# Hashed attention with a feed-forward layer on one core: the first token casts moved up, a load drawn forward, and two more output units summed by DMA

## The chip, the core and the metric

The kernel runs on one core of a Trainium2 chip. The core has five engines with a queue of instructions each: TensorE (PE in the profile), VectorE (DVE), ScalarE (ACT), GpSimd (POOL) and SyncE (SP, which here only issues DMAs). An engine takes its queue in order, so an instruction that waits holds up all that stands behind it. The metric is the device time of one execution in microseconds (us), less is better.

## What is computed

Attention over 4 batches of 8 heads, 768 tokens of 64 numbers each, in which a query sees the keys of its own hash bucket alone, and then a feed-forward layer on all 3072 tokens:

```python
q_bits = (np.einsum('bhsd,dk->bhsk', q, proj) > 0)      # 6 bits, k likewise
mask = q_bucket[:, :, :, None] == k_bucket[:, :, None, :]
scores = np.where(mask, scale * np.matmul(q, k.transpose(0, 1, 3, 2)), -1e9)
attn = np.exp(scores - max); attn = attn / (sum + 1e-09)
x = (attn @ v) as (3072, 512)                           # tokens x (head, dim)
h = x @ w_in                                            # 512 x 2048
out = (h * np.clip(h + 3.0, 0.0, 6.0) / 6.0) @ w_out    # 2048 x 512
```

Inputs and outputs are float32.

## The kernel before

**Precision.** Every matmul works on pairs: a number is rounded (ACT, a cast to fp32r, the high part) and the rest is a subtraction (the low part), and products of high with high, high with low and low with high are added up. So the attention weights p become `ph` (L475) and `pl` (L477 on POOL, L479 on DVE), a token chunk `xr` becomes `xh` (L642) and `xl` (L643).

**Attention.** The 32 heads have 6 tiles of 128 queries each: 192 steps, numbered k or g, head 16 having steps 96 to 101. For a step, TensorE computes scores against all keys (L387, L389), three steps ahead (`lead`), DVE takes the maximum (L396, in `lowest`), ACT the exponential (L408), TensorE transposes p (L418), ACT and DVE split it, and TensorE multiplies with the values into an accumulator `acc` (L500, L512). From step 102 on, p goes by DVE's transposition (L429, "flip") and a round trip by DMA through the tensors `fd`, `spare` and `px`. The hash bits of a head come from six matmuls `z` (L334 to L336) and a comparison on DVE (L352, `bits`). A head's queries and keys (`raw`) are cast and split on POOL two heads ahead (L276, L304, L318). The tile they are written to is the one that the scores of two heads before are computed from.

**Outputs.** An accumulator holds two query tiles (a unit u = 0, 1 or 2 of a head, 256 tokens) as two halves of 64 partitions that have to be summed. `output` copies it whole to a tile `y` (ACT, L542), units 0 and 1 to a tile y0, unit 2 to y2; both tiles exist once (`bufs=1`). The first half is stored to the tensor `xs` by a plain DMA, and the second half added to it there by a DMA of GpSimd that accumulates (`add`, L521). `add` is called in steps with k+3 at 1 or 4 of a head's six, and later on at k at 1 or 3. For the last head of a batch, all three units (of batch 0 the third alone) are summed on the chip instead: ACT copies one half (L539), DVE adds the other (L540), and one store does.

**Feed-forward.** `xs` holds attention before division by the sums. The FFN of batch 0 runs by itself from step 52 on; those of batches 1 to 3 run beside attention from step 101 on (`beside_ffn`), in chunks (b, t) of 256 tokens. A chunk is loaded (`load_x`, four groups of 128 columns, two heads each), the reciprocals of the sums are spread (L570 on POOL), transposed (`rt`, L580, on TensorE), multiplied in (L583, DVE) and the result is split (`split_x`). `there` says when a chunk may begin: when its units are out and no addition to its batch is held. The first chunk, (1, 0), is prepared in steps 94 to 101 and split at the start of step 102 (`opening`), and then TensorE computes h (L653), ACT and DVE the activation (L675, L676) and its split (L681, L682, the operand `gb`), and TensorE the product with w_out (`po`, L691 to L696).

**Order.** PE, DVE, ACT and POOL run in the order in which the code is written, step by step. SP's DMAs are put in order by the framework, which also adds the semaphore waits: for data, and for tiles that are reused. `bank` takes a PSUM bank that an earlier tile has to leave.

The lines are those of the kernel before; in the changed one the same instructions stand 6 or 7 lines lower (L546 for L542, L576 for L570, L586 for L580, L649 for L642). L521 is the same in both.

Of the kernel before, what the change touches and what calls it, by code (L numbers as in the profile page):

```python
# [10 lines left out]
F32 = mybir.dt.float32  # L11
# [7 lines left out]
P = 128  # L19
# [9 lines left out]
LA = 3  # L29
# [14 lines left out]
def lsh_attention_moe(  # L44
# [11 lines left out]
    B, H, D, S = qkT.shape  # L56
    D //= 2
    DM, DF = w_in.shape
    KT = S // P
    HW = S // 2  # L60
    QT = HW // P
    NCC = DM // P
    NFC = DF // P
    TC = 256
# [5 lines left out]
    sp = ctx.enter_context(tc.tile_pool(name="sp", bufs=2))  # L70
# [5 lines left out]
    def dma(out: bass.AP, in_: bass.AP):  # L76
        nonlocal last
        last = nc.sync.dma_start(out=out, in_=in_)
# [4 lines left out]
    spare = []  # L83

    def wide_tile(shape, dtype, name: str):
        nonlocal ob_turn
        tag = "oa" if spare else ("oa", "ob")[ob_turn % 2]
        ob_turn += 1
        return sp.tile(shape, dtype, name=name, tag=tag, bufs=1)
# [301 lines left out]
    def lowest(g: int):  # L391

        s = scs.pop(g)
        m = sp.tile([P, 1], F32, name=f"m{g}", tag="m", bufs=4)
        pr_ = sp.tile([P, 2, HW], F32, name=f"p{g}", tag="p", bufs=2)
        nc.vector.tensor_scalar(  # L396
            out=pr_[:], in0=s[:, :, :HW], scalar1=CAP, scalar2=None,
            op0=ALU.min, op1=ALU.min, accum_out=m[:],
        )
        probs[g] = pr_, m  # L400
# [113 lines left out]
                    start=(part == 0 and kt == 0), stop=(part == 1 and kt == KT - 1),  # L514
                )

    adds = []

    def add():
        for _, to, of in adds:  # L520
            nc.gpsimd.dma_start(out=to, in_=of, accum_op=ALU.add)  # L521
        adds.clear()

    def output(un: int):
        nonlocal vdone
        i, u = divmod(un, KT // 2)
        b, h = divmod(i, H)
        o = (h % 2) * D
        acc = accs.pop(un)

        if u != 1:
            outs[i] = sp.tile([P, 4 * P if u == 0 else 2 * P], F32, name=f"y{i}_{u}", tag=f"y{u}", bufs=1)
        y = outs[i][:, 2 * P :] if u == 1 else outs[i][:, : 2 * P]

        r = slice(o, o + D)
        r2 = slice(D - o, 2 * D - o)
        last_head = h == H - 1 and (b > 0 or u == 2)
        if last_head:
            nc.scalar.copy(y[r], acc[r2])  # L539
            nc.vector.tensor_add(y[r], acc[r], y[r])  # L540
        else:
            nc.scalar.copy(y, acc[:])  # L542
        if u or last_head:
            c = slice(2 * u * P, 2 * (u + 1) * P) if last_head and b else slice(0, 4 * P) if u == 1 else slice(4 * P, S)
            to = xs[b][h * D : (h + 1) * D, c]

            with tc.issue_after(copied.ins):
                dma(out=to, in_=y[r] if last_head else outs[i][r])
            if not last_head:
                adds.append((i, to, outs[i][r2]))  # L550
        vdone = 2 * un + 2


# [44 lines left out]
        if pieces:  # L598
            pieces.pop(0)()

    def load_x(b: int, t: int, ccs: range):
        assert all(not b * H <= a[0] < b * H + ccs.stop * P // D for a in adds)
        ts = slice(t * TC, (t + 1) * TC)
        xr = wide_tile([P, NCC, TC], F32, f"xr{b}_{t}")
        of = xs[b][: len(ccs) * P, ts].rearrange("(cc p) t -> p cc t", p=P)
        if paced:
            for cc in ccs:
                pieces.append(lambda cc=cc: dma(out=xr[:, cc], in_=of[:, cc]))
            piece()
        else:  # L610
            dma(out=xr[:, : len(ccs)], in_=of)
        return xr

    def scale_x(b: int, t: int, ccs: range, xr, rc=None):
# [132 lines left out]
    def load0(t: int, ccs: range):  # L747
        if t not in xr0:
            xr0[t] = wide_tile([P, NCC, TC], F32, f"xr0_{t}")
        assert all(not ccs.start * P // D <= a[0] < ccs.stop * P // D for a in adds)  # L750
        dma(
            out=xr0[t][:, ccs.start : ccs.stop],
            in_=xs[0][ccs.start * P : ccs.stop * P, t * TC : (t + 1) * TC].rearrange("(cc p) t -> p cc t", p=P),
        )
# [75 lines left out]
    def first_ffn(resume):  # L830
# [79 lines left out]
        ffn_on = False  # L910
        yield

    def ffn():
        nonlocal ffn_on, stage
        chunks = [(b, t) for b in range(1, B) for t in range(NTC)]
# [3 lines left out]
        def there(c: int) -> bool:  # L919

            b, t = chunks[c]
            return vdone >= (b + 1) * HK - KT + 2 * (t + 1) and not any(b * H <= a[0] < (b + 1) * H for a in adds)

        def begin(c: int):
            b, t = chunks[c]
            if not spare:
                spare.append(sp.tile([P, 2 * WC], F32, name="spare", tag="ob", bufs=1))
            xr[c] = load_x(b, t, range(NCC))
            todo = scale_x(b, t, range(NCC), xr[c])
            if b < B - 1:  # L930
                side.extend(todo + [lambda: None] * (0 if paced else 2))
                if not paced:
                    opening.append(lambda: (place(c), [split(c, cc) for cc in range(NCC)]))
                return

            side.extend([lambda: None] * (4 if t else 6) + todo[:2])
            for cc in range(NCC):
                side.append(todo[2 + cc])
                side.append(lambda cc=cc: (place(c) if cc == 0 else None, split(c, cc)))
# [147 lines left out]
    with tc.manual_schedule(engines={ET.PE, ET.DVE, ET.Activation, ET.Pool}):  # L1087
# [15 lines left out]
        def beside_ffn(k: int):  # L1103

            nonlocal paced, stage, held
            held = False
            if k < GT:
                for c in range(2):  # L1110
                    transp(k, c)
                exponential(k + 1)
            for _ in range(2):
                u = vnext // 2
                if u < NS // 2 and (2 * u < GT or k % 2 and k >= 2 * u + 3):
                    if vnext % 2 == 0 and k >= GT:
                        value_whole()
                        through.append(u)
                        break
                    if value_half():  # L1120
                        through.append(vnext // 2 - 1)
                if k < GT:
                    break
            if k == GT:
                opening.pop()()
            if k + 2 < NS and k >= GT:
                lowest(k + 2)
            go("A")
            if k < GT:
                for c in range(2):  # L1130
                    split_p(k, c, False)
                split_lows()
                while through:
                    output(through.pop(0))
                flip(k + 1)
            if k + 2 < NS:
                if k < GT:
                    lowest(k + 2)
                exponential(k + 2)
            paced = True  # L1140
            multiply()
            if k + 2 < NS:
                flip(k + 2)
            if GT <= k - LT < NS:
                for c in range(2):
                    split_p(k - LT, c, False)
            split_lows()
            go("B")
            if k == NS + LT:
                homes.clear()  # L1150
            while through and (through[0] < vnext // 2 - 1 or k % 2 == 0 or k < GT):
                output(through.pop(0))
            hashed = k + LA < NS and (k + LA) % KT == 4 and (k + LA) // KT + 1 < NJ
            if hashed:
                hash_qk((k + LA) // KT + 1)
            go("C")
            if hashed:
                bits((k + LA) // KT + 1)
            if k + LA < NS:
                lead(k + LA)  # L1160
            if moves:
                moves.pop(0)()
            if GT <= k + 1 < NS:
                move(k + 1)

            place_in_chunk = (k - GT) % NFC
            if subs and (k % 2 and (k < GT or place_in_chunk != NFC - 1) or k > GT and place_in_chunk == 0):
                subs.pop(0)()
            go("D")
            if k % KT in (1, 3):  # L1170
                add()

        for k in range(NS + LT + 2):
# [6 lines left out]
                lent += lents[cc3:]  # L1180
            if k == GB:
                lent.clear()
            if k == HK:
                late["x"] = sp.tile([P, S], F32, name="late", tag="raw", bufs=1)
            for c in range(2):
# [19 lines left out]
                whole = False  # L1205

            hashed = k >= GF and (k + LA) % KT == 2
            if k >= GF and k + LA < end and not hashed:
                lead(k + LA)
            for c in range(2):  # L1210
                split_p(k, c, third)
            split_lows()
            multiply()
            held = False
            if (k < GF or hashed) and k + LA < end:
                if hashed:
                    if (k + LA) // KT + 1 < NJ:
                        hash_qk((k + LA) // KT + 1)
                        bits((k + LA) // KT + 1)
                    next(fill, None)  # L1220
                lead(k + LA)
# [27 lines left out]
                next(first)  # L1249
        paced = False  # L1250
        assert vnext == NS and not through
        add()
        for _ in fill:
            pass
# [47 lines left out]
```

## Time and profile before

| | us |
|---|---|
| median of 3 runs (977.09 to 977.16) | 977.11 |
| the profiled execution | 976.93 |
| its span | 975.2 |
| mean granted TensorE clock | 0.997 |

| engine | busy us | share of the span |
|---|---|---|
| PE | 951.2 | 98% |
| DVE | 716.8 | 74% |
| ACT | 626.9 | 64% |
| POOL | 480.8 | 49% |

The span runs from the first to the last instruction; the 1.73 us around it belong to the execution too. In the rows of a timeline stand the start, the duration (of the group, if several like instructions follow each other: x6), the engine, the line, what is written and what is read, and in brackets the idle time of the engine before it with what ended it.

### The profile page before, as it was taken

To read this page: it belongs to the slowest core of one execution; us is meant where nothing else is said; L and a number is where in the kernel's file an instruction comes from. 1 tells how busy PE (TensorE), PEld (TensorE's weight loads), DVE (VectorE), ACT (ScalarE), POOL (GpSimd) and SP (SyncE) were. 2 spreads that over 40 slices of the span, in tenths; PEclk is the share of its full clock that TensorE was granted. 3 is DMA by queue.
4 is the path that set the end of the run, shared out by engine and by line. 5 is a ranking of instruction groups with operands and counts; after the bars stand their busy time and mean duration, and the time that the engine had idled before them with its cause. 6 is when DMAs were issued, how large, how long until landed. Compare 5 with 4: busy or idle time off the path is not lost.

```text
span 975.2 us, 19413 instructions
## 1 busy us (share of the span) xinstructions
PE 951.2 (98%) x6306; PEld 875.4 (90%) x6306; DVE 716.8 (74%) x1476; ACT 626.9 (64%) x1421; POOL 480.8 (49%) x498
## 2 busy tenths in 40 slices
PE   8999999999999998899999999999999999999997
PEld 7999888999989998799999889999999899889896
DVE  7999988888569998777777778878777774342422
ACT  6898875656478887567766666676676664333332
POOL 6777744655537775355555546546556542000000
PEclk9999999999999999999999999999999999999999
DMA  3567579100035544688798787788787772101000
GB/s 118 139 163 179 133 237 374 42 2 1 6 118 126 124 111 123 181 249 237 227 258 243 230 245 235 234 264 243 237 266 229 218 225 69 44 1 44 1 22 22
DMA packets 113116, 151.65 MB, mean 156 GB/s; under 512 B 13764, under 2 KB 82116, under 8 KB 113016
## 3 DMA queue, kind: packets, MB, share of 16 engines
q1 hardware_dynamic: 108456, 144.79, 48.7%
q0 software_dynamic: 4560, 5.64, 4.8%
q8 instruction: 50, 0.82, 0.4%
q14 instruction: 50, 0.41, 0.1%
HBM read 77.34 MB, written 53.61 MB: 134 GB/s over the span
## 4 chain that ended last, share of the span: by engine, by line
PE 80%; DVE 9%; issue 3%; POOL 3%; DMA 2%; ACT 2%; SPq 1%; DVEq 0%; ACTq 0%; POOLq 0%
PE h L653 26%; PE po L696 6%; PE po L691 6%; PE po L692 6%; PE acc L500 6%; PE acc L512 6%; PE s L389 5%; PE s L387 5%; PE pt L418 5%; DVE p L396 3%; DVE pl L479 2%; POOL pl L477 2%; DVE qq L352 1%; PE z L334 1%; PE z L335 1%
## 5 line engine op out<-in xcount | busy, mean ns | idle before, releaser
L408 ACT ACTIVATE p<-p,m 128x768 f32<-128x768 f32 x192 | 180.2, 939 | 92.7 <-DVE p L396 87.9
L396 DVE TENSOR_SCALAR_CACHE_REDUCE p<-s 128x768 f32<-128x768 f32 x192 | 182.9, 953 | 40.4 <-PE s L389 24.9
L676 DVE SCALAR_TENSOR_TENSOR h<-g,h 128x256 f32<-128x256 f32 x192 | 81.9, 426 | 95.3 <-ACT g L675 93.4
L675 ACT ACTIVATE g<-h,three 128x256 f32<-128x256 f32 x192 | 91.0, 474 | 91.5 <-PE h L653 89.6
L653 PE MATMUL h<-xh,w 128*128 128x256 f32 x1024 | 147.0, 283 | 1.6 <-ACT xh L642 1.6
L653 PEld LDWEIGHTS h<-xh,w 128*128 128x128 f32 x1024 | 135.7, 189 | 5.1 <-ACT xh L642 1.8
L429 DVE STREAM_TRANSPOSE p<-p 128x768 f32<-128x768 f32 x90 | 88.1, 979 | 60.3 <-ACT p L408 60.3
L477 POOL TENSOR_TENSOR pl<-spare,ph 128x384 fp32r<-128x384 f32 x45 | 62.4, 1388 | 117.7 <-ACT ph L475 82.2
L479 DVE TENSOR_TENSOR pl<-pt,ph 128x384 fp32r<-128x384 f32 x196 | 100.0, 550 | 3.5 <-ACT ph L475 3.0
L681 ACT CAST gb<-h 128x256 fp32r<-128x256 f32 x141 | 52.5, 372 | 77.2 <-DVE h L676 44.0
L387 PE MATMUL s<-kk,qq 76*128 76x384 f32 x384 | 100.1, 341 | 1.8 <-ACT kk L357 1.5
L389 PE MATMUL s<-kk,qq 128*128 128x384 f32 x384 | 100.4, 343 | 0.0
L692 PE MATMUL po<-w,gb 128*128 128x512 f32 x250 | 98.3, 393 | 0.0
L691 PE MATMUL po<-w,gb 128*128 128x512 f32 x250 | 98.3, 393 | 0.0
L477 POOL TENSOR_TENSOR pl<-px,ph 128x384 fp32r<-128x384 f32 x45 | 61.6, 1370 | 72.6 <-ACT ph L475 58.5
L475 ACT CAST ph<-pt 128x384 fp32r<-128x384 f32 x196 | 86.0, 473 | 14.7 <-PE pt L418 12.7
L216 POOL TENSOR_TENSOR w<-wr,w 128x128 fp32r<-128x128 f32 x128 | 72.0, 594 | 45.2 <-ACT w L210 42.1
L418 PE MATMUL pt<-ident,p 128*128 128x128 f32 x612 | 85.9, 274 | 3.6 <-DVE pl L479 2.7
L418 PEld LDWEIGHTS pt<-ident,p 128*128 128x128 f32 x612 | 71.7, 141 | 11.1 <-PE pt L418 2.5
L653 PE MATMUL h<-xl,w 128*128 128x256 f32 x512 | 81.5, 281 | 0.0
L696 PE MATMUL po<-w,gb 128*128 128x512 f32 x250 | 78.8, 396 | 1.5 <-DVE gb L682 1.5
L387 PEld LDWEIGHTS s<-kk,qq 76*128 76x128 f32 x384 | 66.7, 190 | 11.3 <-ACT kk L357 2.1
(153 smaller groups left out, 2133.4 us busy)
## 6 DMA issues: line engine op xcount, KB each, us to landing
fd<-p SPq DMA_DIRECT2D x90, 384.0 KB
spare<-fd SPq DMA_DIRECT2D x180, 96.0 KB
px<-fd SPq DMA_DIRECT2D x180, 96.0 KB
kk<-qq SPq DMA_DIRECT2D x62, 192.0 KB
wr<-in_w_in SPq DMA_DIRECT2D x16, 512.0 KB
wr<-in_w_out SPq DMA_DIRECT2D x16, 512.0 KB
raw<-in_qkT SPq DMA_DIRECT2D x19, 384.0 KB
vr<-in_v SPq DMA_DIRECT2D x32, 192.0 KB
```

What stands on the lines that cost most here:

```text
L387: nc.tensor.matmul(s[:, c, :HW], lhsT=q1[:KM, us], rhs=half(k1[:KM], c), start=True, stop=False)
L389: nc.tensor.matmul(s[:, c, :HW], lhsT=q2[:, us], rhs=half(k2, c), start=False, stop=True)
L396: nc.vector.tensor_scalar(out=pr_[:], in0=s[:, :, :HW], scalar1=CAP, scalar2=None, op0=ALU.min, op1=ALU.min, accum_out=m[:],)
L408: nc.scalar.activation(pr_[:], pr_[:], AF.Exp, bias=m[:], scale=-1.0, accum_out=sms[b][:, t, h : h + 1])
L418: nc.tensor.transpose(pt[:, x], probs[g][0][:, c, x * P : (x + 1) * P], ident[:])
L477: engine.tensor_sub(lo, pt, hi.bitcast(F32))
L479: lows.append(lambda: engine.tensor_sub(lo, pt, hi.bitcast(F32)))
L653: nc.tensor.matmul(hp, lhsT=wi[:, wp, wc], rhs=x[cc][xp], start=(k == 0 and cc == 0), stop=(k == 2 and cc == NCC - 1),)
L675: nc.scalar.activation(r[:], hp, AF.Relu, bias=three[:], scale=1.0)
L691: nc.tensor.matmul(po[u], lhsT=gh[:, us], rhs=wo[:, 0], start=(fc == 0), stop=False)
L692: nc.tensor.matmul(po[u], lhsT=gh[:, us], rhs=wo[:, 1], start=False, stop=False)
L696: nc.tensor.matmul(po[u], lhsT=gl[:, us], rhs=wo[:, 0], start=False, stop=(fc == NFC - 1))
```

## The change

Four edits:

- **Casts.** The split of chunk (1, 0) into `xh` and `xl` (four casts on ACT, four subtractions on DVE) is called in step 101, between the maximum and the exponential of step 103. It was called at the start of step 102, behind that exponential.
- **Load.** Three of the four column groups of chunk (1, 0), heads 8 to 13, are loaded in step 90; `begin` loads the fourth. A chunk may begin when no addition to its own tokens is held (`pending`); before, none to its whole batch might be.
- **Bits.** In step 96, the scores of step 99 and the hash bits of head 17 come behind the low parts and the pending multiplication, as before they came ahead of them.
- **Additions.** For the last heads of batches 1, 2 and 3 (heads 15, 23 and 31) unit 0 alone is summed on the chip. Units 1 and 2 are copied whole, one half is stored, and the other added by an accumulating DMA. These additions are held over one call of `add` (`fresh`). That is six DMAs more for POOL, six L540 fewer for DVE.

```diff
-    adds = []
+    adds, fresh = [], []
 
     def add():
-        for _, to, of in adds:
+        for _, _, to, of in adds:
             nc.gpsimd.dma_start(out=to, in_=of, accum_op=ALU.add)
-        adds.clear()
+        adds[:] = fresh
+        fresh.clear()
...
-        last_head = h == H - 1 and (b > 0 or u == 2)
+        last_head = h == H - 1 and u == (0 if b else 2)
...
         if u or last_head:
-            c = slice(2 * u * P, 2 * (u + 1) * P) if last_head and b else slice(0, 4 * P) if u == 1 else slice(4 * P, S)
+            single = last_head or h == H - 1 and b
+            c = slice(2 * u * P, 2 * (u + 1) * P) if single else slice(0, 4 * P) if u == 1 else slice(4 * P, S)
...
-                dma(out=to, in_=y[r] if last_head else outs[i][r])
+                dma(out=to, in_=y[r] if single else outs[i][r])
             if not last_head:
-                adds.append((i, to, outs[i][r2]))
+                ts = (u,) if single or u else (0, 1)
+                (fresh if single else adds).append((i, ts if u != 1 or single else (0, 1), to, y[r2] if single else outs[i][r2]))
...
+    def load_first_x():
+        spare.append(sp.tile([P, 2 * WC], F32, name="spare", tag="ob", bufs=1))
+        first_x.append(load_x(1, 0, range(cc3)))
...
-            return vdone >= (b + 1) * HK - KT + 2 * (t + 1) and not any(b * H <= a[0] < (b + 1) * H for a in adds)
+            return vdone >= (b + 1) * HK - KT + 2 * (t + 1) and not pending(b, range(H), t)
...
-            xr[c] = load_x(b, t, range(NCC))
+            xr[c] = load_x(b, t, range(NCC) if c else range(cc3, NCC), None if c else first_x[0])
...
-            if k == GT:
-                opening.pop()()
...
                 if k < GT:
                     lowest(k + 2)
+                    assert len(side) <= 2
+                    opening.pop()()
                 exponential(k + 2)
...
+            if k == GF - 6:
+                load_first_x()
...
             hashed = k >= GF and (k + LA) % KT == 2
-            if k >= GF and k + LA < end and not hashed:
+            after = hashed or k >= GF and (k + LA) % KT == 3
+            if k >= GF and k + LA < end and not after:
                 lead(k + LA)
...
-            if (k < GF or hashed) and k + LA < end:
+            if (k < GF or after) and k + LA < end:
```

How the rows move on two engines. First ACT at the end of batch 1: from the copy of head 16's first accumulator (acc48, to y16_0) to the exponential of step 103. `ph49` and `ph50` are high parts, `xh1_0` the cast of chunk (1, 0). Before:

```order
L542 COPY y16_0_5453<-acc48_5410 128x256
L475 CAST ph49_0_5422<-pt99_0_5435 128x3x128
L475 CAST ph49_1_5425<-pt99_1_5439 128x3x128
L408 ACTIVATE p101_5445,sms2_5284<-p101_5445,m101_5444 128x768
L475 CAST ph50_0_5500<-pt100_0_5476 128x3x128
L475 CAST ph50_1_5503<-pt100_1_5480 128x3x128
L408 ACTIVATE p102_5486,sms2_5284<-p102_5486,m102_5485 128x768
L475 CAST ph50_0_5500<-pt101_0_5508 128x3x128
L475 CAST ph50_1_5503<-pt101_1_5512 128x3x128
L542 COPY y16_0_5453<-acc49_5488 128x256
L408 ACTIVATE p103_5533,sms2_5284<-p103_5533,m103_5532 128x768
L642 CAST xh1_0_5562<-xr1_0_5271 128x256 x4
```

And in the changed kernel:

```order
L546 COPY y16_0_5455<-acc48_5409 128x256
L475 CAST ph49_0_5425<-pt99_0_5434 128x3x128
L475 CAST ph49_1_5428<-pt99_1_5438 128x3x128
L408 ACTIVATE p101_5444,sms2_5285<-p101_5444,m101_5443 128x768
L475 CAST ph50_0_5501<-pt100_0_5475 128x3x128
L475 CAST ph50_1_5504<-pt100_1_5479 128x3x128
L408 ACTIVATE p102_5485,sms2_5285<-p102_5485,m102_5484 128x768
L475 CAST ph50_0_5501<-pt101_0_5509 128x3x128
L475 CAST ph50_1_5504<-pt101_1_5513 128x3x128
L546 COPY y16_0_5455<-acc49_5487 128x256
L649 CAST xh1_0_5536<-xr1_0_5092 128x256 x4
L408 ACTIVATE p103_5534,sms2_5285<-p103_5534,m103_5533 128x768
```

The four casts now stand ahead of exponential 103 (the last two rows are exchanged), and the rest is as it was.

GpSimd at the same place: `raw18`, `qq_18` and `kk_18` are head 18's rows, cast and split; `spare` with `rc` is the spreading of the reciprocals; `y15_0` and `y15_2` are head 15's output tiles. Before:

```order
L276 TENSOR_SCALAR raw18_5302<-raw18_5302 64x768
L570 COPY spare_5270<-rc1_0_5273 128x256 x2
L304 CAST qq_18_5456<-raw18_5302 128x768
L318 TENSOR_TENSOR kk_18_5455<-raw18_5302,qq_18_5456 64x768
L318 TENSOR_TENSOR qq_18_5456<-raw18_5302,qq_18_5456 64x768
L477 TENSOR_TENSOR pl51_1_5625<-spare_5270,ph51_1_5624 128x3x128
L367 CAST vv17_5662<-vr17_5332 128x6x64
```

And in the changed kernel:

```order
L276 TENSOR_SCALAR raw18_5304<-raw18_5304 64x768
L576 COPY spare_5091<-rc1_0_5268 128x256
L304 CAST qq_18_5458<-raw18_5304 128x768
L318 TENSOR_TENSOR kk_18_5457<-raw18_5304,qq_18_5458 64x768
L318 TENSOR_TENSOR qq_18_5458<-raw18_5304,qq_18_5458 64x768
L521 DMA xs1_126<-y15_0_5236 64x256
L521 DMA xs1_126<-y15_2_5383 64x256
L477 TENSOR_TENSOR pl51_1_5626<-spare_5091,ph51_1_5625 128x3x128
L367 CAST vv17_5663<-vr17_5345 128x6x64
```

Between head 18's split and the low part `pl51`, the two accumulating DMAs of head 15 have come in, and one spreading copy has gone ahead of these rows.

GpSimd again, where batch 2 ends: `y23_0` is head 23's tile, `xs2` the tensor of batch 2, `pl73` the low part of the attention weights of two steps. In the changed kernel:

```order
L576 COPY spare_5091<-rc2_0_8146 128x256
L477 TENSOR_TENSOR pl73_1_8366<-spare_5091,ph73_1_8365 128x3x128
L318 TENSOR_TENSOR kk_26_8392<-raw26_8187,qq_26_8393 64x768
L576 COPY spare_5091<-rc2_0_8146 128x256
L521 DMA xs2_127<-y23_0_8056 64x256
L477 TENSOR_TENSOR pl73_1_8366<-px_5555,ph73_1_8365 128x3x128
L477 TENSOR_TENSOR pl74_1_8491<-spare_5091,ph74_1_8490 128x3x128
```

Its fifth row is new; before, the low part `pl73_1` from `px` came right behind the spreading copy.

More of the change, by code (lines that the diff above doesn't have):

```diff
@@ L515, in values_whole, with pending @@
                 )
-    adds = []
+    adds, fresh = [], []
     def add():
-        for _, to, of in adds:
+        for _, _, to, of in adds:
             nc.gpsimd.dma_start(out=to, in_=of, accum_op=ALU.add)
-        adds.clear()
+        adds[:] = fresh
+        fresh.clear()
+    def pending(b: int, hs: range, t: int) -> bool:
+        return any(a[0] - b * H in hs and t in a[1] for a in adds + fresh)
     def output(un: int):
@@ L599, in piece, with load_x @@
             pieces.pop(0)()
-    def load_x(b: int, t: int, ccs: range):
-        assert all(not b * H <= a[0] < b * H + ccs.stop * P // D for a in adds)
+    def load_x(b: int, t: int, ccs: range, xr=None):
+        assert not pending(b, range(ccs.start * P // D, ccs.stop * P // D), t)
         ts = slice(t * TC, (t + 1) * TC)
-        xr = wide_tile([P, NCC, TC], F32, f"xr{b}_{t}")
-        of = xs[b][: len(ccs) * P, ts].rearrange("(cc p) t -> p cc t", p=P)
+        if xr is None:
+            xr = wide_tile([P, NCC, TC], F32, f"xr{b}_{t}")
+        of = xs[b][:, ts].rearrange("(cc p) t -> p cc t", p=P)
         if paced:
@@ L610, in load_x @@
         else:
-            dma(out=xr[:, : len(ccs)], in_=of)
+            dma(out=xr[:, ccs.start : ccs.stop], in_=of[:, ccs.start : ccs.stop])
         return xr
@@ L749, in load0 @@
             xr0[t] = wide_tile([P, NCC, TC], F32, f"xr0_{t}")
-        assert all(not ccs.start * P // D <= a[0] < ccs.stop * P // D for a in adds)
+        assert not pending(0, range(ccs.start * P // D, ccs.stop * P // D), t)
         dma(
@@ L911, in first_ffn @@
         yield
+    first_x = []
+    def load_first_x():
+        spare.append(sp.tile([P, 2 * WC], F32, name="spare", tag="ob", bufs=1))
+        first_x.append(load_x(1, 0, range(cc3)))
     def ffn():
@@ L921, in there @@
             b, t = chunks[c]
-            return vdone >= (b + 1) * HK - KT + 2 * (t + 1) and not any(b * H <= a[0] < (b + 1) * H for a in adds)
+            return vdone >= (b + 1) * HK - KT + 2 * (t + 1) and not pending(b, range(H), t)
         def begin(c: int):
             b, t = chunks[c]
-            if not spare:
-                spare.append(sp.tile([P, 2 * WC], F32, name="spare", tag="ob", bufs=1))
-            xr[c] = load_x(b, t, range(NCC))
+            xr[c] = load_x(b, t, range(NCC) if c else range(cc3, NCC), None if c else first_x[0])
             todo = scale_x(b, t, range(NCC), xr[c])
@@ L1251, in lsh_attention_moe @@
         assert vnext == NS and not through
+        add()
         add()
```

## The prediction

> **What bounds the kernel now.** The page first: the engines' busy time and the chain that ended last.
>
> ```profile
> span 975.2 us, 19413 instructions
> PE 951.2 (98%) x6306; PEld 875.4 (90%) x6306; DVE 716.8 (74%) x1476; ACT 626.9 (64%) x1421; POOL 480.8 (49%) x498
> ...
> PE 80%; DVE 9%; issue 3%; POOL 3%; DMA 2%; ACT 2%; SPq 1%; DVEq 0%; ACTq 0%; POOLq 0%
> ```
>
> TensorE is busy for 98% of the span, so only its waits can be taken away, and every new wait of it is paid in full. The profiled execution took 976.93 us, 1.73 more than its span; the median of the runs shown is 977.11, so I make the sum on the first and add 0.18 at the end. The change works in the stretch where attention of batch 1 ends and its FFN begins, so TensorE's timeline from 380 to 414 us comes next, with the idle time before an instruction and its releaser in brackets.
>
> ```profile
> 384.53 0.98 PE L418 MATMUL pt<-ident,p 128*128 128x128 f32 x6 [1.00 <-DVE pl L479]
> ...
> 387.78 0.41 PE L580 MATMUL rt<-ident,spare 128*128 128x128 f32 x2 [0.84 <-DVE y L540]
> ...
> 389.90 0.52 PE L389 MATMUL s<-kk,qq 128*128 128x384 f32 x2
> 390.26 0.38 PE L580 MATMUL rt<-ident,spare 128*128 128x128 f32 x2
> 390.50 0.92 PE L418 MATMUL pt<-ident,p 128*128 128x128 f32 x6
> ...
> 397.72 0.87 PE L512 MATMUL acc<-ph,vv 128*128 128x256 f32 x6
> ...
> 400.91 1.77 PE L653 MATMUL h<-xh,w 128*128 128x256 f32 x8 [1.60 <-ACT xh L642]
> ...
> 404.43 1.91 PE L653 MATMUL h<-xh,w 128*128 128x256 f32 x8
> ...
> 409.95 1.10 PE L653 MATMUL h<-xh,w 128*128 128x256 f32 x8
> ...
> 413.43 0.73 PE L696 MATMUL po<-w,gb 128*128 128x512 f32 x2 [1.01 <-DVE gb L682]
> ```
>
> Three waits belong to the change: 1.00 us for DVE's low part (its queue has the hash bits ahead), 0.84 for the on-chip sum of two output halves, 1.60 for the first token cast. After the 1.60 the same eight matmuls take 1.91 us at 404.43, against 1.10 at 409.95. The table by stretches, whose third column from the right is the granted clock, says why.
>
> ```profile
> 384.00:394.00 10.00, 8.39 (x60) 7.25 (x60) 8.07 (x19) 5.97 (x13) 5.61 (x7) 1.00 0.36 110
> 400.00:410.00 10.00, 9.09 (x45) 8.35 (x46) 6.92 (x14) 6.03 (x16) 0.24 (x1) 0.83 0.80 254
> ```
>
> A clock of 0.83 over 10 us is 1.7 us of lost rate.
>
> **The change, part by part.** ScalarE (ACT) is the engine on which it hangs; these are its rows of before, then GpSimd's (POOL).
>
> ```profile
> 392.17 0.37 ACT L542 COPY y<-acc 128x256 f32<-128x256 f32 x1 [1.22 <-PE acc L500]
> ...
> 399.53 0.93 ACT L408 ACTIVATE p<-p,m 128x768 f32<-128x768 f32 x1 [1.96 <-DVE p L396]
> ...
> 400.46 1.31 ACT L642 CAST xh<-xr 128x256 fp32r<-128x256 f32 x4
> 404.47 0.94 ACT L408 ACTIVATE p<-p,m 128x768 f32<-128x768 f32 x1 [2.69 <-DVE p L396]
> ```
>
> ```profile
> 387.23 2.14 POOL L276 TENSOR_SCALAR raw<-raw 64x768 f32<-64x768 f32 x1 [3.16 <-DMA raw<-in_qkT]
> 389.32 0.39 POOL L570 COPY spare<-rc 128x256 f32<-128x256 f32 x1
> ...
> 391.12 0.83 POOL L304 CAST qq<-raw 128x768 fp32r<-128x768 f32 x1
> ...
> 393.94 1.84 POOL L318 TENSOR_TENSOR qq<-raw,qq 64x768 fp32r<-64x768 f32 x1
> ```
>
> *Gains ahead.* Bits behind low parts, and no sum in front of the transposes of 1/denominator: 1.00 + 0.84 = 1.84 us earlier. The matmuls of 390.50 then start at 388.66, and head 16's first accumulator, whose copy stood at 392.17, is full at 390.33.
>
> *Token columns loaded at step 90.* SP issues 384 of 512 KB earlier; nobody waits for them, and the DMA share was 0.36 in the row above: nothing. Left at its old place is a load of 128 KB. Head 18's raw rows, queued behind it, may land sooner than at 387.23. If that cover were gone, the load would delay the reciprocal's product on DVE, at most back to what it is now.
>
> *Sums by DMA.* DVE loses six additions, ACT copies 128 rows for 64 in the same time, POOL gains six issues. But the copy has a new wait. Tile y0 is single: head 16's copy (L546 in the changed code, L542 in the row above) may not overwrite the tile before head 15's accumulating DMA has read it and landed. That DMA is queued on POOL behind head 18's cast and its two low parts (L304, L318, L318). The cast needs head 16's last score matmuls to be done, which I put at 389.90 + 0.52 + 0.24 (the reciprocal's transposes now stand ahead of them) - 1.84 = 388.8; and, if the raw rows land no sooner, it starts at 389.32 + 0.39 = 389.7. I take 389.1. From its start to the end of the last low part it is 393.94 + 1.84 - 391.12 = 4.66 us, so the DMA is issued at 393.8 (393.5 to 394.4). How long such a DMA takes from issue to landing stands in the view of tensor xs, first for 353 to 384 us, then for 600 to 700 us.
>
> ```profile
> L521 POOL DMA_DIRECT2D xs<-y x4: 835/860/892, 354.3 to 377.4; - x4
> ...
> DMA to landing us min/median/max: 2.6/2.9/3.1
> ```
>
> ```profile
> L521 POOL DMA_DIRECT2D xs<-y x6: 827/842/848, 633.2 to 696.0; - x6
> ...
> DMA to landing us min/median/max: 2.6/3.8/4.3
> ```
>
> Half as large as the bigger of these, the first lands 2.6 to 3.1 us after issue; with 2.7 the copy runs at 396.6, not at 390.33. Behind it on ACT stand the casts of step 99 and the exponentials; TensorE's next transposes need the accumulator's bank. So TensorE stands still for about 6.3 us, and the copy is 4.4 us behind its place of before (392.17). By the page "DMA: Bandwidth & Descriptors" of the Trainium skill, section "Anatomy of one DMA", a GpSimd DMA costs 2.0 us plus bytes over 436 KB/us, by which estimate 64 KB takes 2.2 us and the stall would be 0.5 shorter; the trace's shortest is 2.6, so I don't use it.
>
> *Casts ahead of the exponential.* From the copy to L512 it was 397.72 - 392.17 = 5.55 us; so L512 starts at 402.1, the casts 0.45 later (half of that row's hi matmuls), at 402.6, and end at 403.9. Then come exponential 103 (0.93), and on DVE its transposition and the next maximum, whose group rows are:
>
> ```profile
> L396 DVE TENSOR_SCALAR_CACHE_REDUCE p<-s 128x768 f32<-128x768 f32 x192 | 182.9, 953 | 40.4 <-PE s L389 24.9
> ...
> L429 DVE STREAM_TRANSPOSE p<-p 128x768 f32<-128x768 f32 x90 | 88.1, 979 | 60.3 <-ACT p L408 60.3
> ```
>
> 403.9 + 0.93 + 0.98 + 0.95 + 0.1 for handing over = 406.9 for exponential 104, against 404.47: +2.4. Everything from there to the wait at 413.43 is a chain of ACT and DVE, so what 104 loses, TensorE loses; behind 413.43 it runs without a wait that could give it back.
>
> *The clock.* A gap of 1.60 cost 1.7 us of rate; a gap of 6.3 must cost some too. Before, that loss lay beside the ACT chain and so ended nothing; now it falls on 397 to 402, where TensorE sets the pace: 0 to 1.7, taken as 1.1. The page "TensorE: Matmul & The Clock Gate" of the skill, section "What's actually happening", gives half rate after an idle window of about 3.4 us; the trace shows it already after a 1.60 gap. By that rule, too, the long gap is throttled. Batch 1 in all: 2.4 + 1.1 = **+3.5** (2.2 to 5.0, the upper end with the late cast and the landing of 3.1).
>
> *The same copy in batch 2.* POOL's accumulating DMA for head 23 comes right behind a spread copy:
>
> ```profile
> 615.87 0.40 POOL L570 COPY spare<-rc 128x256 f32<-128x256 f32 x1
> ```
>
> and head 24's copy, the activation of the FFN, the exponential and the next chunk's casts queue up behind each other on ACT, while TensorE needs the casts at 622.72:
>
> ```profile
> 616.80 0.37 ACT L542 COPY y<-acc 128x256 f32<-128x256 f32 x1
> ...
> 621.25 1.31 ACT L642 CAST xh<-xr 128x256 fp32r<-128x256 f32 x4
> ```
>
> ```profile
> 622.72 1.10 PE L653 MATMUL h<-xh,w 128*128 128x256 f32 x8
> ```
>
> Issued at 616.3, landed at 618.9 to 620.6, 620.1 by the median of 3.8: the copy is 3.3 us late. The last cast ends at 622.56 and is wanted by about 623.5, a slack of 1.0. So **+2.3** (1.1 to 2.8). The third units (y2) and batch 3 have only later, idler copies, and their adds go where POOL has time: 0, at most +1.
>
> Sum: 976.93 + 3.5 + 2.3 = 982.7; on the median's scale **982.9 us**. With both lower ends 980.4, with both upper ends 985.9.
>
> **Rivals.**
>
> *A, no stall: faster.* If head 15's DMA landed by 390.3, the copy would go on time: 1.84 gained, the casts at 397.72 - 1.84 + 0.45 = 396.3, ahead of exponential 103, which stood at 399.53 and comes at 397.7. Then 104 comes at 397.7 + 3.0 = 400.7, 3.8 before 404.47: **973.3**. For it: the three waits are real. Against it: the order puts the DMA behind 4.66 us of POOL work. The point that decides is the copy's start: 104 shifts by the copy's shift less 2.0, so it is a loss from a copy at 394.2 on; landing would have to be by 394.1, when the DMA has hardly been issued.
>
> *B, batch 1 alone.* In batch 2 ACT catches up because the landing is as short as 2.6 and TensorE has other matmuls to do: 982.9 - 2.3 = **980.6**.
>
> *C, more throttle.* The 2.3 us stall in batch 2 is longer than the 1.60 that was followed by the lower clock: another 1.7, **984.6**. The skill's rule of a whole idle window speaks against this rival, the row at 404.43 for it.
>
> *D, no change.* Gains and stalls cancel (copy at 394.2 in batch 1 and cover in batch 2): 977.
>
> **How the numbers follow.** Forecast 0.53, B 0.15, C 0.14, A 0.13, D 0.05. Forecast, B and C hold 0.82 and together reach from 979.3 (B with batch 1's lower end: 977.1 + 2.2) to 985.9. A measurement tells about 0.2%, 2 us, from no change: slower 0.82, same 0.05, faster 0.13.
>
> **What would show it.** In the changed kernel's profile: ACT's copy of 128x256 near 396 us, with several us of idle before it released by a DMA of xs; TensorE idle by about 6 us at 390; a clock below 1 in 390:410; the wait of 1.60 for the cast gone, as those of 1.00 and 0.84; a second stall of about 2 us at 617 to 624. It is wrong if the copy at 390 has no idle time before it (then A), or if the casts run ahead of exponential 103 and TensorE still waits for something else there.

## The result, and the profile after

The changed kernel takes 985.42 us (985.08 to 987.30, 4 runs) against 977.13 for the kernel before (977.09 to 977.99, 4 runs): a ratio of 1.0087, with a 95% interval of 1.0069 to 1.0104, so 8.3 us or 0.87% slower. The page of its profiled execution (985.08 us) has nearly the same work on TensorE (953.1 us busy, 951.2 before) in a longer span, and DMA has risen in the chain that ended last from 2% to 4%, issue from 3% to 4%:

```profile
span 983.3 us, 19408 instructions
PE 953.1 (97%) x6306; PEld 876.1 (89%) x6306; DVE 715.5 (73%) x1470; ACT 626.6 (64%) x1421; POOL 482.9 (49%) x504
...
PE 75%; DVE 8%; issue 4%; DMA 4%; POOL 4%; SPq 2%; ACT 2%; DVEq 0%; POOLq 0%; ACTq 0%
```

What TensorE waited for from 370 to 430 us (in total, how often, the longest): the 1.60 for the first cast and the 0.84 for the sum on the chip are gone, for DVE's low part it still waits 0.3, and one wait is larger than all that went.

```profile
PE rt L586 <- ACT y L546: 7.8, 2, 7.3
PE po L703 <- DVE gb L689: 1.1, 1, 1.1
PE po L698 <- ACT gb L688: 0.7, 1, 0.7
PE pt L418 <- DVE pl L479: 0.3, 1, 0.3
```

In TensorE's timeline the long one stands behind the last matmul of head 16's first accumulator. (The shorter one in the same group, 0.55 us at 386.02, is for the copy of head 15's last unit; it stands where the sum on the chip was.)

```profile
390.52 0.52 PE L500 MATMUL acc<-pl,vv 128*128 128x256 f32 x3
398.30 0.66 PE L586 MATMUL rt<-ident,spare 128*128 128x128 f32 x2 [7.26 <-ACT y L546]
```

TensorE waits for ACT's copy `y`; so the next view is ACT's timeline, to see what the copy itself waited for, and then POOL's.

```profile
397.79 0.37 ACT L546 COPY y<-acc 128x256 f32<-128x256 f32 x1 [7.93 <-issue]
...
406.15 1.33 ACT L649 CAST xh<-xr 128x256 fp32r<-128x256 f32 x4 [0.69 <-PE acc L512]
407.39 0.94 ACT L408 ACTIVATE p<-p,m 128x768 f32<-128x768 f32 x1
...
410.45 0.94 ACT L408 ACTIVATE p<-p,m 128x768 f32<-128x768 f32 x1 [2.04 <-DVE p L396]
```

```profile
389.56 0.83 POOL L304 CAST qq<-raw 128x768 fp32r<-128x768 f32 x1
...
394.10 1.75 POOL L521 DMA_DIRECT2D xs<-y  x2
```

ACT stood idle for 7.93 us before the copy. The profile names no releaser ("issue"), and TensorE's last matmul of that accumulator had ended at 391.0; such a gap is one to look up in the order of the instructions. There the last reader of tile y0 ahead of the copy is head 15's accumulating DMA. It was issued at 394.10, behind L304 and the two L318, and the first of the two landed 3.6 us later, at 397.7, just before the copy started:

```profile
L521 POOL DMA_DIRECT2D xs<-y x2: 897/1008/1119, 394.1 to 394.7; - x2
...
DMA to landing us min/median/max: 3.6/3.7/3.9
```

The table by stretches shows the idle TensorE and the clock behind it (third column from the right). Its last three rows are a finer cut: the clock is at half from 396.2 to 403.0, and TensorE works for 4.7 us of that.

```profile
384.00:394.00 10.00, 6.49 (x49) 5.71 (x47) 6.31 (x13) 3.98 (x9) 7.14 (x6) 1.00 0.39 114
394.00:400.00 6.00, 1.70 (x6) 1.67 (x7) 1.35 (x3) 2.06 (x5) 1.85 (x3) 0.68 0.41 89
400.00:410.00 10.00, 10.00 (x64) 9.64 (x63) 7.35 (x15) 5.38 (x13) 0.00 (x0) 0.85 0.19 60
...
391.10:396.20 5.10, 0.00 (x0) 0.00 (x0) 0.23 (x2) 0.00 (x0) 4.68 (x4) 1.00 0.58 136
396.20:398.30 2.10, 0.00 (x0) 0.03 (x1) 0.00 (x0) 0.51 (x2) 0.00 (x0) 0.50 0.85 202
398.30:403.00 4.70, 4.70 (x20) 4.60 (x21) 2.79 (x7) 2.83 (x7) 0.00 (x0) 0.50 0.01 2
```

In batch 2 the same two rows, with the releaser named this time: head 24's copies for tile y0 and, 20 us later, for y2.

```profile
624.59 0.37 ACT L546 COPY y<-acc 128x256 f32<-128x256 f32 x1 [2.45 <-DMA xs<-y]
...
644.88 0.37 ACT L546 COPY y<-acc 128x256 f32<-128x256 f32 x1 [1.15 <-DMA xs<-y]
```

To see where in the program the time came from, the starts of ACT's exponentials (L408) of six steps are compared over all profiled executions; the last three columns are the time from one step to another, less the same in the kernel before. Step 96 is ahead of the change's stretch, 98 ahead of the stall, 104 behind batch 1's end, 150 and 160 around batch 2's end. The runs e1 to e9 are the experiments below.

```
run                 96      98      104     150     160     191     96-98  98-104  150-160
before              377.03  381.88  404.47  615.05  661.68  802.17
changed             378.11  382.45  410.45  620.29  669.93  810.36   -0.5    +5.4     +3.0
e1 sum on chip      376.98  381.84  401.62  612.72  659.35  800.07    0.0    -2.8      0.0
e2 batch 1 on chip  378.18  383.04  402.82  613.47  663.42  804.45    0.0    -2.8     +3.3
e3 first not held   377.23  381.57  400.85  611.81  659.21  800.07   -0.5    -3.3     +0.8
e4 adds alone       376.99  381.33  411.72  622.25  672.00  812.51   -0.5    +7.8     +3.1
e5 casts late       378.12  382.46  402.96  613.33  659.35  799.95   -0.5    -2.1     -0.6
e6 bits early       377.94  382.28  403.09  613.42  660.85  802.23   -0.5    -1.8     +0.8
e7 filled wait      378.97  383.32  409.32  619.71  669.14  809.64   -0.5    +3.4     +2.8
e8 ahead of split   377.56  381.91  402.67  612.30  662.49  803.94   -0.5    -1.8     +3.6
e9 batch 1 only     377.68  382.02  401.30  611.86  658.87  799.55   -0.5    -3.3     +0.4
```

From step 98 the changed kernel loses 5.4 us in batch 1; 0.5 it had gained just before, as every run does in which head 15's second unit is no longer summed on the chip, so from step 96 the loss is 4.9. In batch 2 it loses 3.0. At step 96, ahead of all this, the executions lie from 0.1 us ahead of the kernel before to 1.9 behind it (the changed kernel 1.1 behind), and from 104 to 150, where the code is the same, they drift against it by -1.0 to +0.5. So single traces are compared by these differences and not by their ends, and a difference of less than 1 us in a single trace shows nothing by itself.

### The profile page after: what moved, and what is told of

The parts are those of the page before. It is cut to its first block, busy times and chain, and to the rows that moved or that the text cites. A ratio compares the mean times of both kernels' runs of the same rounds, so it can differ in the third digit from the quotient of the medians.

```text
span 983.3 us, 19408 instructions
## 1 busy us (share of the span) xinstructions
PE 953.1 (97%) x6306; PEld 876.1 (89%) x6306; DVE 715.5 (73%) x1470; ACT 626.6 (64%) x1421; POOL 482.9 (49%) x504
## 4 chain that ended last, share of the span: by engine, by line
PE 75%; DVE 8%; issue 4%; DMA 4%; POOL 4%; SPq 2%; ACT 2%; DVEq 0%; POOLq 0%; ACTq 0%
PE h L660 24%; PE acc L500 6%; PE po L703 6%; PE po L698 6%; PE po L699 6%; PE pt L418 5%; PE acc L512 5%; PE s L389 5%; PE s L387 5%; DVE p L396 3%; SPq L78 2%; POOL pl L477 2%; DVE pl L479 2%; DMA px<-fd 2%; ACT ph L475 1%
## 5 line engine op out<-in xcount | busy, mean ns | idle before, releaser
L408 ACT ACTIVATE p<-p,m 128x768 f32<-128x768 f32 x192 | 180.2, 939 | 88.9 <-DVE p L396 81.0
```

The costliest lines, as they stand in the source:

```text
L408: nc.scalar.activation(pr_[:], pr_[:], AF.Exp, bias=m[:], scale=-1.0, accum_out=sms[b][:, t, h : h + 1])
```

## The experiments

Three theories were set against each other. S: output copies wait for the accumulating DMA to leave the tile. M: the moved casts and bits cost. P: the six more GpSimd DMAs cost by themselves, whatever waits for them. Each run is timed against the kernel before on its own chip, so ratios are compared, not times.

**e1: the sums back on the chip.**

```diff
-        last_head = h == H - 1 and u == (0 if b else 2)
+        last_head = h == H - 1 and (b > 0 or u == 2)
```

> The changed kernel with the last heads' units summed on the chip again (the fourth edit undone), the other three edits kept. Theory S (head 16's and head 24's output copies wait until the accumulating DMA has left tile y0): no such wait is left, ACT's copy at 390 us and at 617 us have no idle time before them, and the time is 977.1 - 3.8 + about 0.6 of drift seen ahead of the stretch = 974 us (973 to 976). Rival M (the casts in front of the exponential and the moved hash bits are what costs): stays at 983 to 986. Rival P (six more GpSimd issues and their traffic cost by themselves): 974, as S, so this run doesn't tell P from S.

Measured: 974.74 us against 977.60, ratio 0.9977 (0.9966 to 0.9988). ACT's copy follows its accumulator, with the same 1.22 us of idle time as in the kernel before:

```profile
390.97 0.37 ACT L546 COPY y<-acc 128x256 f32<-128x256 f32 x1 [1.22 <-PE acc L500]
```

M falls: without the fourth edit the other three are a gain of about 2.3 us by the ratio.

**e2: batch 1 alone back on the chip.** Heads 23 and 31 keep their DMAs.

```diff
-        last_head = h == H - 1 and u == (0 if b else 2)
+        last_head = h == H - 1 and (b == 1 or u == (0 if b else 2))
```

> The changed kernel with head 15's units summed on the chip, those of heads 23 and 31 by DMA. S: batch 1's stall goes, batch 2's stays; by the shift of the exponentials in the changed kernel's trace (5.4 us up to step 104, 3.0 us at steps 150 to 157) it is 974 + 3.0 = 977 us. If batch 2's loss were an echo of batch 1's: 974. M: 983 to 986.

Measured: 979.30 us, ratio 1.0009 (0.9998 to 1.0020), which is over the 977 expected. Against e1 on the same chip it is 3.1 us more by the ratios and 4.6 by the medians. Batch 2's loss stands by itself (3.3 in the table, 0.0 in e1); what ACT waited for from 612 to 660 us has it:

```profile
ACT y L546 <- DMA xs<-y: 3.6, 2, 2.4
```

By the two ratios, batch 1's part is 1.0087 - 1.0009, or 7.6 us (7.7 by the table from step 96: 4.9 of loss, and 2.8 of gain not had).

**e3: the same DMAs, but unit 1's not held over one call.**

```diff
-                (fresh if single else adds).append((i, ts if u != 1 or single else (0, 1), to, y[r2] if single else outs[i][r2]))
+                (fresh if single and u == 2 else adds).append((i, ts if u != 1 or single else (0, 1), to, y[r2] if single else outs[i][r2]))
```

> The changed kernel, the same DMAs, but unit 1's addition is not held over a call of add: it is issued one call earlier, ahead of head 18's split in batch 1 and one spreading copy earlier in batch 2, and unit 2's as before. S: both copies find tile y0 free, 974 us (973 to 976). P: as many issues and as much traffic as in the changed kernel, so 984 to 986. M: 983 to 986.

Measured: 974.75 us, ratio 0.9971 (0.9960 to 0.9983). The edit holds for heads 15, 23 and 31. Head 15's DMA is now issued by POOL ahead of head 18's rows, 4 us before the copy, which finds its tile free:

```profile
386.20 0.83 POOL L521 DMA_DIRECT2D xs<-y  x1
```

```profile
390.20 0.37 ACT L546 COPY y<-acc 128x256 f32<-128x256 f32 x1 [1.22 <-PE acc L500]
```

P falls with this one: as many DMAs of the same size, and 11 us less than the changed kernel by the ratios (1.0087 - 0.9971 = 0.0116). It is when the DMA is issued that counts.

**e4: the fourth edit alone, on the kernel before.**

> The kernel before with the fourth edit alone. S: the stall stands at 392 us there, the DMA is issued at 395.8 and lands 3.6 later, the copy is 7.3 us late, and the casts come behind exponential 103 as before; with batch 2's 3.0 the time is 986 to 989 us. M: 977. P: 977 plus six issues, under 983.

Measured: 988.63 us, ratio 1.0114 (1.0096 to 1.0133), inside what S gave. The copy came at 398.25, 6.1 us behind its place in the kernel before and not the 7.3 expected, but the clock stayed lower for longer (0.84 from 400 to 410 us, 0.86 from 410 to 420). TensorE's waits from 370 to 425 us are the changed kernel's stall and two waits of the kernel before, side by side:

```profile
PE rt L586 <- ACT y L546: 7.8, 2, 7.3
PE h L659 <- ACT xh L648: 1.6, 1, 1.6
PE pt L418 <- DVE pl L479: 1.5, 2, 1.2
```

**e5 and e6: e3 with one of the other edits undone.** In e5 the casts are back at the start of step 102:

```diff
+            if k == GT:
+                opening.pop()()
...
-                    assert len(side) <= 2
-                    opening.pop()()
```

In e6 the bits are back ahead of the low parts:

```diff
-            after = hashed or k >= GF and (k + LA) % KT == 3
+            after = hashed
```

> The kernel of e3 (unit 1's addition not held) with the first edit undone: the first token casts stand again behind exponential 103. The prediction's step gave this edit 3.8 - 1.84 = 2.0 us: 974.75 + 2.0 = 976.8 us, and TensorE's wait of 1.6 us for the first cast comes back with a clock below 1 behind it. If the casts' place is worth nothing once the sum on the chip is gone: 974.8.

> The kernel of e3 with the third edit undone: scores of step 99 and the hash bits of head 17 come again ahead of the low parts. The prediction's step gave it the 1.00 us wait for DVE's low part: 975.8 us. If DVE makes it up before anything is needed: 974.8.

Measured: e5 975.03 us, ratio 0.9981 (0.9971 to 0.9991); e6 976.42, ratio 0.9990 (0.9979 to 1.0001); e3 had 0.9971. The casts' place is worth 1.2 us at step 104 by the table, less than the 2.0 of the sum. Whether any of it is left at the end is not shown: by the ratios it is 1.0 us with intervals that overlap, and in the traces e5 starts its last exponential no later than e3 (799.95 and 800.07), although it lay 0.9 us further back at step 96. The wait for the first cast and the lower clock behind it did come back in e5:

```profile
PE h L660 <- ACT xh L649: 1.7, 1, 1.7
```

```profile
400.00:410.00 10.00, 9.92 (x52) 9.16 (x53) 8.06 (x17) 5.57 (x15) 1.74 (x2) 0.83 0.84 264
```

but there TensorE then works through at the lower rate, while with the casts in front it waits for `gb` instead (1.1 and 0.7 us, as in the rows of the changed kernel). The bits' place is worth 1.9 us by the ratios, again with intervals that overlap, and 1.5 by the table, where the sum had 1.00. No run undoes the second edit, the earlier load, by itself. Of the 3.8 us that e3 gains from step 96 to 104, the casts have 1.2, the bits 1.5, and the sums by DMA 1.0 (e1, with the sums on the chip, gains 2.8); that leaves the load about nothing.

**e7: TensorE kept busy during the stall.** The last six matmuls of the accumulator are repeated eight times.

```diff
+        if (u, c) == (48, 1):
+            for n in range(8 * 2 * QT):
+                x = n % QT
+                nc.tensor.matmul(
+                    acc[:], lhsT=vv[:, QT + x], rhs=(hi, lo)[n // QT % 2][:, x],
+                    start=False, stop=n == 8 * 2 * QT - 1,
+                )
```

> The changed kernel with 48 extra matmuls of 0.147 us each, about 7 us, in the gap: the last six matmuls of head 16's first accumulator are repeated eight times, added up, so that unit's output is another than the reference's. The copy still waits for the DMA to 397.8, but TensorE is busy meanwhile. If the lower clock behind the gap made the 2.4 us by which copy to casts took longer than the 6.0 of the sum, the clock stays at 1.00 and the time is 985.4 - 2.4 = 983.0 us (982.5 to 984). If the stretch is paced by ACT and DVE alone, the clock costs nothing: 985.4.

Measured: 984.02 us, ratio 1.0070 (1.0048 to 1.0092), 1.7 us under the changed kernel, with overlapping intervals. The trace is clearer. The extra matmuls ended at 397.7, sooner than expected, and the copy still started with the landing (issue at 395.0 plus 3.6), whatever the bracket names. The clock stayed at 1.00, and copy to casts took 404.93 - 398.67 = 6.3 us, where the changed kernel took 406.15 - 397.79 = 8.4:

```profile
398.67 0.37 ACT L553 COPY y<-acc 128x256 f32<-128x256 f32 x1 [7.95 <-PE acc L507]
...
404.93 1.33 ACT L656 CAST xh<-xr 128x256 fp32r<-128x256 f32 x4 [0.70 <-PE acc L519]
```

```profile
394.00:400.00 6.00, 4.48 (x37) 4.31 (x36) 0.54 (x2) 1.33 (x4) 2.78 (x3) 1.00 0.57 125
400.00:410.00 10.00, 10.00 (x75) 9.50 (x74) 8.56 (x19) 6.79 (x16) 0.00 (x0) 1.00 0.29 98
```

So the lower clock cost 2.1 us of batch 1's loss; the table's 3.4 for 5.4 says the same. It is the price of an idle TensorE over and above the idle time.

**e8: the held addition called right ahead of head 18's split.**

```diff
+        if j == GT:
+            add()
         if t == 0 and n < NJ:
```

> The changed kernel with the same held addition called once more, right ahead of head 18's split on GpSimd: the DMA is issued at 389.5 in place of 394.1, and lands at 392.5 to 393.1. S says that the loss follows the landing: the copy runs at about 393, 1 us behind its place in the kernel before, which the casts' new place (2.0) more than pays in batch 1, less 0 to 2.4 of clock; batch 2's 3.1 stays: 977.1 - 1.0 + 1.2 + 3.1 = 980.4 us (979 to 982). If what counts is that the DMA is held over at all: 985.4.

Measured: 979.30 us, ratio 1.0020 (1.0009 to 1.0031): 2.0 us over the kernel before, inside S's range. The loss follows the landing, here 2.5 us after issue, and the copy starts with it:

```profile
388.84 1.76 POOL L521 DMA_DIRECT2D xs<-y  x2
```

```profile
391.44 0.37 ACT L546 COPY y<-acc 128x256 f32<-128x256 f32 x1 [2.12 <-PE acc L500]
```

In batch 1 it is a gain already (1.8 us from step 98, 2.3 from step 96), although the DMA is still held over; batch 2's 3.6 turn it into a loss. The bracket names the accumulator; but in e3, with the same edit of the casts and bits, the idle time there was 1.22, and the copy's start is 0.1 us behind the landing (388.84 + 2.5).

**e9: what the experiments point to.** e3, with batches 2 and 3 summed on the chip.

```diff
-        last_head = h == H - 1 and u == (0 if b else 2)
+        last_head = h == H - 1 and (b > 1 or u == (0 if b else 2))
```

> The kernel of e3 with the last heads of batches 2 and 3 summed on the chip as before; only head 15's units 1 and 2 go by DMA, unit 1's not held over. S: no output copy waits for a DMA anywhere, neither at 390 nor at 615 to 645, where e3 lost 1.1 us to the third unit's tile; TensorE's wait for the sum on the chip in batch 1 (1.1 us in e1) is gone as well. 974.75 - 1.1 = 973.7 us, a ratio of about 0.996. If the third unit's wait is covered: as e3, 0.997.

Measured over five rounds: 974.53 us against 977.23, ratio 0.9974 (0.9965 to 0.9984). Its trace has no copy that waits for a DMA, and lies 2.6 us under the kernel before at the last exponential, against 2.1 in e1 and e3. But by the ratios e1, e3 and e9 cannot be told apart: all three beat both kernels, by 0.23 to 0.29% over the kernel before. So the sum by DMA, where nobody waits for it, gains 1.0 us up to step 104 in the traces (3.8 from step 96 in e3 and e9, 2.8 in e1), but nothing that shows in the times. Nor was the 973.7 expected reached.

One test of S was not made: a tile of its own for the last heads' outputs, which would take the wait away by another buffer.

## Why the prediction was right, and where its terms were off

The direction and the mechanism held. The time lay inside the range (979.3 to 985.9), at its upper end: the loss was 8.3 us for 5.8. The upper ends of the two terms alone give 984.9; the rest of the range is the "at most +1" for the third units and batch 3. Of the two profiled executions' difference, 8.15 us, 1.08 was there at step 96 already, ahead of the change's stretch; "less drift" below means less these 1.08.

- *Gains ahead, 1.84.* From step 96 to 99 the changed kernel's exponentials gain 2.0 us. The parts were otherwise: the bits alone are worth 1.5 there (e6), more than the 1.00 given, and the sum on the chip 0.4 to 0.6 (e6's gain that is left, and e3 against e1), less than the 0.84.
- *When the DMA is issued, 393.8.* It was at 394.10, or 393.0 less drift, 0.8 sooner than forecast. Head 18's raw rows were scaled (L276) at 386.94, which less drift is 1.4 sooner than before, as the prediction had thought possible. The chain of L304 and two L318 (4.66 us) held to 0.1.
- *Its landing, 2.7 us after issue.* Mis-sized: 3.6. It was outside the rows that I took it from (2.6 to 3.1). e8's, 5 us earlier in the program, took 2.5 again. SP issues two loads of `raw` at the same moment in the changed kernel, but that they made the difference was not tried.
- *The copy at 396.6.* At 397.79, or 396.7 less drift. That it fits is luck: 0.8 too late at the issue and 0.9 too short at the landing cancel.
- *The clock, 1.1 (0 to 1.7).* Mis-sized: 2.1 by e7, beyond the range given. The upper end was the one loss of 1.7 in the kernel before. Behind the long gap the clock was at half for twice as long (396.2 to 403.0), and the 4.7 us of it in which TensorE worked are 2.35 us of lost rate.
- *Exponential 104, 2.4 + 1.1 behind.* 5.98 behind, of which 1.08 was there at step 96: 4.9 for 3.5. Of the 1.4 more, 1.0 is the clock and 0.3 the way from copy to casts (6.3 at full clock, in e7, for 6.0).
- *Batch 2, 2.3.* 3.0. The copy for y0 waited 2.45 us, less than the 3.3 given, but there was no slack of 1.0 to take off: at the next exponential, step 151, the shift was 2.6. That is the step of this term that failed. "y2 has only idler copies: 0" failed too, as that copy waited 1.15 us; what this cost is not settled, since from 150 to 160 the runs in which only y2's copy waits lie at +0.8, -0.6 and +0.8 (e3, e5, e6), and those in which none waits at 0.0 and +0.4 (e1, e9).
- *Rival A, 973.3 without the stall.* e3 has no stall in batch 1, and from step 96 its step 104 comes 3.8 us earlier, as the rival had it. Up to the last exponential its trace keeps 2.3 of that: 0.8 goes in batch 2 and 0.4 each from 104 to 150 and behind 160, amounts that single traces do not settle.
- *Rival B, batch 1 alone.* It fell: the five runs in which head 24's copy waits for tile y0 lose 2.8 to 3.6 us from 150 to 160, the others 0.8 at most.
- *Rival C, more throttle in batch 2.* The clock was 1.00 from 614 to 644 in the changed kernel's trace: it did not come. The 2.45 us were ACT's wait; TensorE itself stood idle for no more than 0.5 us at a time. There the trace is with the rule of the page "TensorE: Matmul & The Clock Gate" of the Trainium skill (section "What's actually happening"), which lists half rate after at least one idle window of about 3.4 us; the gap of 1.60 us in the kernel before is not.
- *The point that decides: a copy at 394.2.* It held to about 1 us. Less the 0.53 that e8 lay behind at step 96, its copy, at 391.44, is 3.3 us on the good side; batch 1 gained 2.3 from there. The changed kernel's, at 396.7 less drift, is 2.5 on the bad side, and with the 2.1 of clock that makes 4.6 for the 4.9 lost.

## What to carry to other kernels

Work that is moved to another queue takes its place behind what stands in that queue. So before looking at the cost of the work itself, look at each tile that it reads and that exists only once: who wants to write that tile next, and when will the moved work have left it? One accumulating DMA of each last head, issued one call earlier, made the difference between 985.4 and 974.8 us. When TensorE stands idle for several microseconds, add what the clock takes afterwards (here 2.1 us for a gap of 7.3), and check it by filling the gap with matmuls that nobody needs.

## What the hardware showed that was not expected

How long a gap has to be to lower the clock does not follow from its length in these runs. The kernel before and e5 had gaps of 1.6 and 1.7 us, each followed by a mean clock of 0.83 over 10 us. In finer stretches of the kernel before, the clock is still 1.00 for the 2.1 us behind its gap (which ended at 400.91), and then at half for about 3.4:

```profile
401.00:403.10 2.10, 2.10 (x12) 1.63 (x13) 1.88 (x5) 0.78 (x3) 0.00 (x0) 1.00 0.98 360
403.10:406.60 3.50, 3.50 (x16) 3.50 (x17) 2.04 (x4) 1.66 (x4) 0.00 (x0) 0.51 0.57 169
406.60:410.00 3.40, 3.40 (x20) 3.12 (x20) 2.59 (x6) 2.59 (x6) 0.24 (x1) 1.00 0.88 280
```

e8 had a gap of 1.45 us, in TensorE's timeline, with the clock at 1.00 in the stretch behind it and in the next, to 410:

```profile
391.95 0.41 PE L586 MATMUL rt<-ident,spare 128*128 128x128 f32 x2 [1.45 <-ACT y L546]
```

```profile
394.00:400.00 6.00, 6.00 (x46) 5.73 (x44) 5.47 (x13) 4.92 (x12) 1.26 (x1) 1.00 0.48 133
```

In the kernel before and e5, the first eight matmuls behind the gap are held back by the casts (1.77 us, where eight such take 1.10); in e8 other matmuls stand there, which wait for nothing. Whether that decides was not tried.

And accumulating DMAs of the same 64 KB took 2.5 us from issue to landing in one place (e8 at 388.8) and 3.6 in another (the changed kernel at 394.1).
